# Gated linear attention with token and channel mixing: one rotating pool of eight PSUM banks, small mixing units between chunk steps, and SBUF-only work on GpSimd

## The chip, the cores and the metric

The kernel runs on one core of a Trainium2 chip. The metric is device time of one execution in microseconds (us), lower is better. The time of an execution is 2 to 3 us longer than the span of the trace that is shown beside it, because the span counts from the first to the last instruction.

Engine names in the profile: PE is TensorE (matrix products), PEld its weight loads, DVE is VectorE, ACT is ScalarE, POOL is GpSimd, SP is SyncE. A clock figure is the share of TensorE's full speed that was granted. `L172` is line 172 of the kernel in question. PSUM is the memory into which PE writes its products, here eight banks; SBUF is the working memory that holds the other tiles. An eviction is the copy of a product from PSUM to SBUF, here by VectorE or ScalarE. The line numbers of the changed kernel and of its variants differ by two or three.

## The reference

There are four batches (b = 0 to 3). Each is a gated linear attention with 8 heads, 768 time steps and head size 48, followed by a two-stage mixer with shared weights:

```python
f = 1.0 / (1.0 + np.exp(-f_logit))
for t in range(S):                                     # S = 768
    state = f[:, :, t, :, None] * state + k_t (outer) v_t
    y[:, :, t] = q_t @ state
x = y as (B, 768, 384)
h  = relu(x^T @ w_tok1) @ w_tok2                       # 768 -> 256 -> 768, over time steps
u  = x + h^T
out = u + relu(u @ w_ch1) @ w_ch2                      # 384 -> 1536 -> 384, over channels
```

Both kernels compute the recurrence in 6 chunks of 128 time steps: the logarithms of the gates (each kept as a bf16 value `Lhi` and its remainder `Llo`) are summed inside a chunk by a triangular matrix product, q and k are scaled by the exponentials of those sums (`qh`, `kh`), `qh` and `kh` are transposed on PE, their products are the scores of a chunk, and a small state is handed from chunk to chunk. `state_bd`, `x_bf` and `u_bf` are bf16 copies of the state, of the attention's output x and of the mixer's u. The mixing of batch b is computed while the attention of batch b+1 runs, so PE has two streams to interleave. The last mixing has nothing beside it.

## The kernel before

A bank of PSUM belongs to one purpose each: five to attention, three to the mixing, in turn. q, k, v and the weights are loaded (and cast to bf16) through GpSimd's queue, f through SyncE's.

```python
ps_S = pt([128, 512], FP32, "ps_S")
ps_AT = [pt([128, 4, 128], FP32, f"ps_AT{p}") for p in range(2)]
ps_y = pt(...); ps_dg = pt(...)
ps_moe = [pt([128, 512], FP32, f"ps_moe{i}") for i in range(3)]      # mixing

def g_lo():                                                          # all arithmetic on ACT and DVE
    nc.vector.tensor_tensor(Llo[ib][...], fbc, Lhi[ib][...], ALU.subtract)

def attn_chunk(b, c, mid=(), front_next=None):
    ...
    nc.vector.tensor_tensor(qh[i][:, :, 0:D], q_sb[ib][:, :, c, :], G[i][:, :, 0:D], ALU.mult)
    nc.vector.tensor_tensor(kh[i][:, :, 0:D], k_sb[ib][:, :, c, :], Gi[i][:, :, 0:D], ALU.mult)
    # PE: transposes of qh and kh to ps_AT[0], ps_AT[1]
    nc.scalar.copy(qkT[i][:, 0:4, :], ps_AT[0])
    nc.vector.tensor_copy(qkT[i][:, 4:8, :], ps_AT[1])               # L186
    # PE: scores from qkT                                            # L191
    front_next()                       # sums of the next chunk
    for m in mid: m()                  # one sixth of the previous batch's mixing
    # masking, readout, state ... (cut)

load_batch_inputs(0, 0, 2); load_batch_inputs(0, 2, NCH)             # 18 loads on GpSimd's queue
load_batch_inputs(1)                                                 # q, k, v of batch 1
load_weights()                                                       # w_tok1, w_tok2, w_ch1, w_ch2
```

## Time and profile before

The median is 242.74 us (two runs, 242.68 and 242.79). The span of the trace is 240.4 us at a mean PE clock of 0.979.

First the page of the kernel before: busy time by engine, and rows of the table of 40 slices (each digit is the busy share of 6 us in tenths).

```profile
PE 183.6 (76%) x1673; PEld 111.5 (46%) x1688; DVE 152.1 (63%) x341; ACT 137.2 (57%) x262; POOL 40.1 (17%) x39
...
PE   0413376103858999999999999999999999989993
...
POOL 9823910821302100150300000000000000000000
...
DMA  8999999999999900099490000121000002100022
```

PE is nearly always busy from slice 14 on, and busy for less than half of the time before it, while the DMA row stands at 8 to 9. So the kernel has two parts: a start held by loads, and a long stretch bound by PE.

Next the table of windows of the same run: duration, then busy time (and instructions) of PE, PEld, DVE, ACT and POOL, PE's clock, DMA share and GB/s. I cut the span where the first scores of a batch start on PE: 78.0 us for batch 1, 119.9 for batch 2, 163.6 for batch 3.

```profile
78.00:119.90 41.90, 40.03 (x401) 24.44 (x403) 35.16 (x78) 23.68 (x56) 6.92 (x4) 1.00 0.93 70
119.90:163.60 43.70, 42.09 (x419) 25.96 (x424) 33.98 (x81) 24.06 (x59) 0.48 (x1) 1.00 0.34 44
163.60:240.40 76.80, 70.09 (x575) 41.89 (x577) 44.41 (x98) 34.63 (x79) 0.00 (x0) 1.00 0.09 32
```

In batch 2's stage PE is busy 42.1 of 43.7 us. Why it idles so little can be seen in PE's timeline (start, duration, engine, line, what): between the transpose of `kh` (L184) and the scores (L191), which must wait for the eviction on VectorE, PE computes other things.

```profile
132.38 0.39 PE L184 MATMUL ps_AT_123<-ident,kh_95 128*128 128x128 bf16 x4
...
132.80 0.33 PE L215 MATMUL ps_dg<-v_sb_81,kh_95 128*128 128x96 bf16 x4
133.39 0.65 PE L280 MATMUL ps_moe_135<-uT,w_ch_75 128*128 128x384 bf16 x3 [0.25 <-DVE zT L285]
133.87 0.33 PE L280 MATMUL ps_moe_133<-uT,w_ch_75 128*128 128x384 bf16 x1
134.13 0.23 PE L191 MATMUL ps_AT_122<-qkT_97 48*128 48x128 bf16 x1
```

In the start, PE's longest wait is for the first weights, and GpSimd's timeline shows why they are late: they were issued after v of batch 1, whose issue had itself stood 11.26 us.

```profile
PE ps_moe_134 L247 <- DMA w_tok_73<-in_moe_w_tok_dram: 12.2, 1, 12.2
```

```profile
28.49 2.21 POOL L78 DMA_DIRECT2D k_sb_80<-in_k_dram  x1
41.96 2.22 POOL L79 DMA_DIRECT2D v_sb_82<-in_v_dram  x1 [11.26 <-issue]
44.17 0.83 POOL L62 DMA_DIRECT2D w_tok_73<-in_moe_w_tok_dram  x1
```

### The profile page before, as it was taken

The page shows a single profiled execution, that of the slowest core. Times are in us where ns is not written, and L with a number is a line of the kernel's source. Part 1 is how long each engine was busy: PE and PEld are TensorE (multiplying, and loading weights), DVE is VectorE, ACT ScalarE, POOL GpSimd, SP SyncE. Part 2 cuts the span into 40 slices and gives each one's busy share as a digit, 9 for nine tenths or more (in the row PEclk, how much of TensorE's full clock was granted, in tenths as well). Part 3 has the DMA queues.
Part 4 walks back from the last instruction along what each step waited for, and adds up shares of the span by engine and source line. Part 5 has one row for each costly group of instructions (what it writes and reads, how often), then busy time and mean ns, then how long its engine had stood idle before and what let it go on. Part 6 is the DMA issues. An engine that isn't in the chain of part 4 may idle for free.

```text
span 240.4 us, 4273 instructions
## 1 busy us (share of the span) xinstructions
PE 183.6 (76%) x1673; PEld 111.5 (46%) x1688; DVE 152.1 (63%) x341; ACT 137.2 (57%) x262; POOL 40.1 (17%) x39
## 2 busy tenths in 40 slices
PE   0413376103858999999999999999999999989993
PEld 0201253001535555566565555666556556546661
DVE  4323769300965999995489998637999872444221
ACT  5479999900697765870376777008776710556300
POOL 9823910821302100150300000000000000000000
PEclk9999999999965999999999999999999999999999
DMA  8999999999999900099490000121000002100022
GB/s 113 147 185 151 163 158 137 174 144 198 208 182 137 103 3 0 3 85 174 135 104 0 3 1 3 65 100 35 0 3 0 3 33 102 64 0 0 8 107 85
DMA packets 91539, 19.93 MB, mean 83 GB/s; under 512 B 80896, under 2 KB 91136, under 8 KB 91520
## 3 DMA queue, kind: packets, MB, share of 16 engines
q0 software_dynamic: 77168, 10.23, 78.3%
q1 hardware_dynamic: 14352, 9.44, 18.4%
q8 instruction: 13, 0.21, 0.4%
q14 instruction: 6, 0.05, 0.1%
HBM read 25.17 MB, written 4.72 MB: 124 GB/s over the span
## 4 chain that ended last, share of the span: by engine, by line
PE 34%; DVE 26%; DMA 15%; issue 9%; ACT 8%; POOL 7%; DVEq 0%; POOLq 0%
DMA q_sb_77<-in_q_dram 6%; DMA w_tok_73<-in_moe_w_tok_dram 6%; PE ps_moe_135 L298 5%; PE ps_moe_133 L298 5%; PE ps_moe_134 L298 5%; PE ps_moe_133 L280 3%; DMA out_dram<-out_sb_132 3%; DVE zT L285 3%; PE ps_moe_134 L280 3%; PE ps_moe_135 L280 3%; DVE u_nat L256 2%; DVE qkT_98 L186 2%; DVE AmT_99 L200 2%; DVE uT L270 2%; DVE state L225 2%
## 5 line engine op out<-in xcount | busy, mean ns | idle before, releaser
L298 PEld LDWEIGHTS <-zT 128*128 128x128 bf16 x288 | 27.7, 98 | 18.3
L280 PEld LDWEIGHTS <-w_ch_75 128*128 128x128 bf16 x288 | 26.5, 97 | 19.9 <-issue 4.5
L280 PE MATMUL ps_moe_133<-uT,w_ch_75 128*128 128x384 bf16 x96 | 22.9, 325 | 1.4 <-DVE uT L270 0.5
L280 PE MATMUL ps_moe_135<-uT,w_ch_75 128*128 128x384 bf16 x96 | 22.6, 325 | 0.8 <-DVE zT L285 0.5
L280 PE MATMUL ps_moe_134<-uT,w_ch_75 128*128 128x384 bf16 x96 | 22.2, 325 | 0.5 <-DVE zT L285 0.3
L220 ACT ACTIVATE x_nat_105<-ps_y 128x384 f32<-128x384 f32 x12 | 6.0, 499 | 24.8 <-PE ps_y L210 24.2
L298 PE MATMUL ps_moe_134<-w_ch_76,zT 128*128 128x384 bf16 x96 | 17.3, 326 | 0.0
L200 DVE TENSOR_TENSOR AmT_100<-ps_AT_122,tri_bf 128x512 bf16<-128x512 f32 x12 | 8.3, 688 | 14.2 <-PE ps_AT_123 L191 14.0
L298 PE MATMUL ps_moe_135<-w_ch_76,zT 128*128 128x384 bf16 x96 | 17.1, 326 | 0.0
L298 PE MATMUL ps_moe_133<-w_ch_76,zT 128*128 128x384 bf16 x96 | 17.1, 326 | 0.0
L287 ACT ACTIVATE zT<-ps_moe_134 128x384 bf16<-128x384 f32 x22 | 10.9, 496 | 8.0 <-PE ps_moe_134 L280 7.8
L161 PE MATMUL ps_dg<-ones_bf,Lhi_85 128*128 128x1 bf16 x40 | 3.5, 166 | 13.5 <-ACT Lhi_85 L143 6.7
L287 ACT ACTIVATE zT<-ps_moe_135 128x384 bf16<-128x384 f32 x22 | 11.0, 500 | 4.9 <-PE ps_moe_135 L280 4.8
L220 ACT ACTIVATE x_nat_104<-ps_y 128x384 f32<-128x384 f32 x12 | 5.8, 486 | 13.9 <-PE ps_y L210 13.9
L247 PE MATMUL ps_moe_134<-x_bf_106,w_tok_73 128*128 128x384 bf16 x6 | 2.5, 452 | 14.1 <-DMA w_tok_73<-in_moe_w_tok_dram 12.2
L247 PEld LDWEIGHTS <-w_tok_73 128*128 128x128 bf16 x48 | 4.6, 105 | 17.9 <-DMA w_tok_73<-in_moe_w_tok_dram 12.4
L287 ACT ACTIVATE zT<-ps_moe_133 128x384 bf16<-128x384 f32 x20 | 10.0, 500 | 4.3 <-PE ps_moe_133 L280 4.2
L224 DVE TENSOR_TENSOR state<-state,ps_dg 48x192 f32<-48x192 f32 x20 | 6.8, 342 | 8.5 <-ACT qkT_98 L185 4.9
L257 ACT ACTIVATE u_bf<-u_nat 128x384 bf16<-128x384 f32 x24 | 11.0, 519 | 1.8 <-DVE u_nat L256 1.6
L200 DVE TENSOR_TENSOR AmT_99<-ps_AT_122,tri_bf 128x512 bf16<-128x512 f32 x12 | 8.2, 685 | 6.0 <-PE ps_AT_123 L191 5.7
L175 ACT ACTIVATE glast<-ps_dg 128x4 f32<-128x4 f32 x20 | 3.6, 178 | 14.1 <-DVE state L227 12.7
L191 PE MATMUL ps_AT_122<-qkT_97 48*128 48x128 bf16 x48 | 5.1, 232 | 7.3 <-ACT qkT_97 L185 5.5
(149 smaller groups left out, 470.3 us busy)
## 6 DMA issues: line engine op xcount, KB each, us to landing
out_dram<-out_sb_131 SPq DMA_DIRECT2D x12, 192.0 KB, 1.9
out_dram<-out_sb_132 SPq DMA_DIRECT2D x12, 192.0 KB, 1.9
f_sb_83<-in_f_logit_dram SPq DMA_DIRECT2D x6, 192.0 KB, 5.7
q_sb_78<-in_q_dram POOLq DMA_DIRECT2D x2, 576.0 KB, 12.6
k_sb_80<-in_k_dram POOLq DMA_DIRECT2D x2, 576.0 KB, 18.2
v_sb_82<-in_v_dram POOLq DMA_DIRECT2D x2, 576.0 KB, 11.6
w_ch_75<-in_moe_w_ch_dram POOLq DMA_DIRECT2D x1, 1152.0 KB, 20.3
w_ch_76<-in_moe_w_ch_dram POOLq DMA_DIRECT2D x1, 1152.0 KB, 24.9
```

Of the source, the lines that this page charges most:

```text
L186: nc.vector.tensor_copy(qkT[i][:, 4:8, :], ps_AT[1])
L191: nc.tensor.matmul(ps_AT[par][:, hp, :], lhsT=qkT[i][rows, 4 + hp, :], rhs=qkT[i][rows, hp, :], start=True, stop=True)
L200: nc.vector.tensor_tensor(AmT[i][:, 0:4, :], ps_AT[0], tb4, ALU.mult)
L220: nc.scalar.activation(x_nat[ib][:, c, :], yflat, AF.Copy, bias=0.0, scale=1.0)
L224: nc.vector.tensor_tensor(state[0:D], state[0:D], ps_dg[0:D, :, 0:D], ALU.add)
L225: nc.vector.tensor_tensor(state[64:64 + D], state[64:64 + D], ps_dg[64:64 + D, :, D:2 * D], ALU.add)
L247: nc.tensor.matmul(pm[:, 0:DM], lhsT=w_tok1[:, kt, rt * 128:(rt + 1) * 128], rhs=x_bf[ib][:, kt, :], start=(kt == 0), stop=(kt == NCH - 1))
L257: nc.scalar.activation(u_bf[:, stt, :], u_nat[:, stt, :], AF.Copy, bias=0.0, scale=1.0)
L280: nc.tensor.matmul(pm[:, 0:384], lhsT=w_ch1[:, kt, cc * 128:(cc + 1) * 128], rhs=uT[:, kt, th * 384:(th + 1) * 384], start=(kt == 0), stop ...
L285: nc.vector.tensor_scalar(dst, pm[:, 0:384], 0.0, None, ALU.max)
L287: nc.scalar.activation(dst, pm[:, 0:384], AF.Relu, bias=0.0, scale=1.0)
L298: nc.tensor.matmul(pm[:, 0:DM], lhsT=zT[:, kt, tt * 128:(tt + 1) * 128], rhs=w_ch2[:, kt, :], start=(kt == 0), stop=(kt == 11))
```

## The change

The kernel was rewritten with five intentions: all PSUM tiles come from one pool of eight banks in rotation, so that neither stream is short of banks; the mixing is cut into 44 small units, spread over four places of each chunk step; the state and the sums are kept compact (384 instead of 512 columns, no padded products); a single activation table is preloaded; and work that touches SBUF alone goes to GpSimd, which was 17% busy. The weights are loaded before batch 1, and f of batch 1 goes through GpSimd's queue too.

The core of the diff, with cuts:

```diff
-    ps_S = pt([128, 512], FP32, "ps_S")
-    ps_AT = [pt([128, 4, 128], FP32, f"ps_AT{p}") for p in range(2)]
-    ...
-    ps_moe = [pt([128, 512], FP32, f"ps_moe{i}") for i in range(3)]
+    ps = ctx.enter_context(tc.tile_pool(name="ps", bufs=8, space=bass.MemoryType.PSUM))
+    def bank(name):
+        return ps.tile([128, 512], FP32, tag="bank", name=name)
+    nc.scalar.preload_act_table_set("natural_log_exp_and_others")
 ...
-            nc.scalar.activation(Lhi[ib]..., fbc, AF.Copy, bias=0.0, scale=1.0)
-            nc.vector.tensor_tensor(Llo[ib]..., fbc, Lhi[ib]..., ALU.subtract)
+        nc.vector.tensor_copy(Lhi[i]..., fbc)
+        nc.gpsimd.tensor_tensor(Llo[i]..., fbc, Lhi[i]..., ALU.subtract)
 ...
-        nc.vector.tensor_tensor(kh[i]..., k_sb[ib][:, :, c, :], Gi[i]..., ALU.mult)
+        nc.gpsimd.tensor_tensor(kh[j]..., k_sb[i][:, :, c, :], Gi[j], ALU.mult)
 ...
-        nc.scalar.activation(x_bf[ib][:, c, :], yflat, AF.Copy, bias=0.0, scale=1.0)
+        nc.gpsimd.tensor_copy(x_bf[i][:, c, :], x_nat[i][:, c, :])
+            nc.gpsimd.tensor_copy(u_bf[:, tt, :], u_nat[:, tt, :])
+        nc.gpsimd.tensor_copy(state_bd[j]..., s...)          # two of them
 ...
-    load_batch_inputs(1)
-    load_weights()
+    for w, src in ((w_tok1, ...), (w_tok2, ...), (w_ch1, ...), (w_ch2, ...)):
+        nc.gpsimd.dma_start(out=w, in_=...)
+    load_f(1, nc.gpsimd)
+    load_qkv(1)
 ...
+            scores(b, c)      # transposes, evictions, scores, masking
+            mix()             # a few units of the previous batch's mixing
+            front(b, c + 1)
+            mix()
+            update(b, c)
+            mix()
+            readout(b, c)
+            mix()
```

The kernel as changed is called "after" below.

## The prediction

> **What bounds the kernel now.** The table of windows splits the 240.4 us span into five stages. (1) 0–71 us: loading and batch 0's attention; PE is busy 26 us of it. The DMA row reads 8–9 tenths throughout, and the list of waits has PE waiting 12.2 us for w_tok until 58.2 us, because the weights were issued (44–47 us in GpSimd's timeline) behind batch 1's q, k, v. (2) 71–119.6 us: batch 1's attention with batch 0's mixing, 48.6 us, of which 10 us ran at half clock. (3) and (4) 119.6–205.2: 43.7 and 41.9 us, PE busy 96%. Start-to-start issue distances there (matmul timeline: 162 ns per 384 columns, 56 per 128) sum to about 28 us of mixing and 11 us of attention per batch, so only 3–4 us are idle. In 120–150 VectorE is 90% busy; in 150–162 PE runs the second channel product alone. (5) 205.2–240.4: the last mixing, 35.2 us, almost pure PE.
>
> **Removed.** 11 table loads of 1283 ns on ACT (about 14 us; the Trainium skill, "ScalarE: Activation LUTs", section "Table sets: the hidden batching unit", says natural_log_exp_and_others holds both functions). On VectorE per batch: kh 2.1, Llo 2.6, state casts 3.1, one state add of each pair 1.7, uT 1.7, against zT +2.2 and the Lhi cast +2: about 7 us of 34 less. ACT loses x_bf 3.0, u_bf 3.1, Lhi 2.1, some zT, and gains uT 2.9. PE loses only about 0.6 us per batch (384 instead of 512 columns in the front).
>
> **Added to GpSimd,** per batch 20–25 us. Estimate from the Trainium skill, "GPSIMD Engine Reference", section 3.1 (about 2.6 cycles per element for two inputs at 1.2 GHz): kh about 1 us against 0.35 on VectorE, Llo about 5 against 2.55. No GpSimd arithmetic of this kind is in this trace.
>
> **On the critical path.** Steady stages are PE-bound: small units let the second channel product fill VectorE-bound gaps, 43.7 to about 41 each; batch 1's stage to about 42 (less cold clock); the tail to about 33.5 (transposes by row tile start earlier). Together about 156 us after batch 1's first chunk, against 169.
>
> **The start decides.** The weights now precede batch 1's loads, which removes the 12 us wait. DMA packets: a batch's q, k or v (6144 packets) takes about 5 us alone, the weights about 17, so w_tok lands by 30 us, all weights by 43, f(1) 49, q(1) 54, k(1) 59, v(1) 64. Hence batch 1 can't start before about 60 us. But Llo and kh of batch 0 now sit on GpSimd, behind whatever DMA issues precede them there. Before, v(1)'s issue stood 11.3 us waiting ("issue") and went out only after q(1) had landed. If all 26 issues come first, GpSimd is held until about 56 us, batch 0's attention starts then, cold and GpSimd-bound, and batch 1 starts at about 85 us: total about 241. If the arithmetic slips in between, about 217. I take both as likely.
>
> **Predicted: 226 us, 8 in 10 between 208 and 246. Faster by over 2%: 0.67; within 2%: 0.16; slower by over 2%: 0.17.**
>
> **What would show it.** Right: no wait for w_tok; one table load; PE 95% or more busy from batch 1's start; VectorE under 80% busy there; that stretch 40–42 us per batch. Start: GpSimd's timeline tells whether the first Llo precedes the last load's issue; if not, PE idles to 50 us or later with GpSimd as releaser. Batch 1's first scores near 60 or 85 us.
>
> **What would make it wrong.** GpSimd elementwise much slower than the estimate, so that kh or state_bd ends chunk steps; GpSimd blocked in mid-kernel by issuing loads of batches 2 and 3 (2.2 us each); banks taken in rotation so that one slow eviction holds PE; gates of batch 1 in ACT's queue waiting for the later f(1).

## The result, and the profile after

| | median us | runs | ratio to before, 95% interval |
|---|---|---|---|
| before | 242.74 | 242.68, 242.79 | |
| after | 274.38 | 273.35, 275.4 | 1.1303 [1.1122, 1.1485] |

The change made the kernel 13% slower. A ratio here and below is the mean time of one kernel's runs over that of the other's runs of the same rounds, so it is not quite the ratio of the medians that are quoted. Executions over 1.5% slower than the fastest of the same kernel are left out of the means.

The page of the kernel after:

```profile
PE 183.5 (68%) x1768; PEld 112.3 (41%) x1768; DVE 136.1 (50%) x254; ACT 104.7 (39%) x221; POOL 122.0 (45%) x167
...
PE   0100000138857879888876788998878999889995
...
POOL 9789002795596887331945433232243323140000
```

PE does the same work (183.5 us against 183.6), VectorE and ScalarE do less, as intended, and the span is 31 us longer. PE idles through most of the first eight slices, and then stands mostly at 7 to 8 tenths where it stood at 9.

The windows, cut in the same way at the first scores of each batch (60.9, 90.9, 140.5 and 191.9 us):

```profile
0.00:60.90 60.90, 4.44 (x52) 2.55 (x54) 10.19 (x22) 14.49 (x27) 38.65 (x43) 1.00 1.83 157
60.90:90.90 30.00, 22.22 (x256) 13.36 (x256) 21.21 (x36) 20.19 (x39) 20.60 (x27) 1.00 0.61 78
90.90:140.50 49.60, 43.42 (x442) 27.01 (x442) 34.84 (x60) 20.77 (x47) 28.80 (x36) 1.00 0.82 58
140.50:191.90 51.40, 42.81 (x442) 26.81 (x442) 28.94 (x57) 20.63 (x47) 17.49 (x30) 0.97 0.49 50
191.90:271.40 79.50, 70.57 (x578) 42.58 (x578) 40.95 (x79) 28.59 (x61) 16.51 (x33) 0.98 0.09 33
```

Where the 31.0 us went, stage by stage:

| stage | before | after | difference |
|---|---|---|---|
| start, up to the first scores of batch 1 | 78.0 | 90.9 | +12.9 |
| batch 1 | 41.9 | 49.6 | +7.7 |
| batch 2 | 43.7 | 51.4 | +7.7 |
| batch 3 and last mixing | 76.8 | 79.5 | +2.7 |

**The start.** GpSimd's timeline after shows that its first arithmetic, `Llo` (L128), stands behind all 26 load issues in its order:

```profile
45.49 2.22 POOL L116 DMA_DIRECT2D k_sb_81<-in_k_dram  x1 [17.95 <-issue]
49.19 2.21 POOL L116 DMA_DIRECT2D v_sb_83<-in_v_dram  x1 [1.48 <-issue]
51.42 5.54 POOL L128 TENSOR_TENSOR Llo_88<-f_sb_84,Lhi_86 128x384 bf16<-128x384 f32 x6
...
58.52 0.90 POOL L155 TENSOR_TENSOR kh_96<-k_sb_80,Gi_92 128x384 bf16<-128x384 bf16 x1
```

The Trainium skill, "PSUM — Partial Sum Buffer", section "Engine vs sequencer instructions", calls GpSimd's queue strictly first in, first out; this trace agrees: ScalarE had finished the gates of batch 0 by 14.9 us, yet `Llo` came after the last issue, and PE's list of waits (total, times, longest) puts 39.0 us of one wait on it. In the same time ScalarE stood 30.24 us at the first gate of batch 1, because f of batch 1 was queued behind the weights:

```profile
PE pt L141 <- POOL Llo_88 L128: 40.8, 5, 39.0
```

```profile
45.12 1.58 ACT L125 ACTIVATE f_sb_85<-f_sb_85 128x768 f32<-128x768 f32 x2 [30.24 <-DMA f_sb_85<-in_f_logit_dram]
```

**The steady batches.** PE's timeline after, in batch 2: nothing stands between the transposes of `kh` (L166) and the scores (L172), so PE waits the whole eviction on VectorE.

```profile
160.34 0.39 PE L166 MATMUL pk<-ident,kh_96 128*128 128x128 bf16 x4
161.52 0.23 PE L172 MATMUL pA_1592<-qkT_98 48*128 48x128 bf16 x1 [0.79 <-DVE qkT_98 L167]
...
161.85 1.64 PE L245 MATMUL pm<-uT,w_ch_76 128*128 128x384 bf16 x9
```

In batch 2's stage this wait appears six times, once per chunk, 0.8 us each; with one wait of 3.0 us for `x_bf` and one of 0.8 us for `u_bf`, both on GpSimd, that is 8.6 of the stage's 8.6 idle us on PE (51.4 less 42.8). Before, PE idled 1.6 us there.

```profile
PE pm L222 <- POOL x_bf_111 L191: 3.0, 1, 3.0
PE pA_1940 L172 <- DVE qkT_99 L167: 0.8, 1, 0.8
```

### The profile page after: what moved, and what is told of

The parts are those of the page before. It is cut to its first block, busy times and chain, and to the rows that moved or that the text cites. A ratio compares the mean times of both kernels' runs of the same rounds, so it can differ in the third digit from the quotient of the medians.

```text
span 271.4 us, 4457 instructions
## 1 busy us (share of the span) xinstructions
PE 183.5 (68%) x1768; PEld 112.3 (41%) x1768; DVE 136.1 (50%) x254; ACT 104.7 (39%) x221; POOL 122.0 (45%) x167
## 4 chain that ended last, share of the span: by engine, by line
PE 57%; POOL 16%; DVE 11%; issue 11%; DMA 3%; ACT 1%; POOLq 0%; DVEq 0%
PE pm L245 18%; PE pm L256 18%; DMA k_sb_80<-in_k_dram 3%; PE pm L222 3%; DVE qkT_99 L167 3%; DVE qkT_98 L167 3%; POOL Llo_88 L128 3%; PE pk L166 2%; POOL u_bf L232 2%; PE pS L150 2%; PE pm L229 2%; PE py L182 2%; PE pd L200 1%; PE pS L151 1%; POOL q_sb_78 L118 1%
## 5 line engine op out<-in xcount | busy, mean ns | idle before, releaser
L245 PE MATMUL pm<-uT,w_ch_76 128*128 128x384 bf16 x288 | 53.0, 331 | 0.0
L256 PE MATMUL pm<-w_ch_77,zT 128*128 128x384 bf16 x288 | 50.0, 326 | 0.0
L251 ACT ACTIVATE zT<-pm 128x384 bf16<-128x384 f32 x48 | 23.6, 492 | 26.1 <-PE pm L245 25.7
L249 DVE TENSOR_SCALAR zT<-pm 128x384 bf16<-128x384 f32 x48 | 26.5, 554 | 11.7 <-PE pm L245 11.1
L141 PEld LDWEIGHTS <-Llo_88 128*128 128x128 bf16 x40 | 2.5, 100 | 42.0 <-POOL Llo_88 L128 41.9
L259 DVE TENSOR_TENSOR out_sb_118<-u_nat,pm 128x384 f32<-128x384 f32 x12 | 6.6, 554 | 16.3 <-PE pm L256 16.3
L232 POOL CAST u_bf<-u_nat 128x384 bf16<-128x384 f32 x24 | 11.3, 503 | 6.0 <-DVE u_nat L231 5.9
L167 DVE CAST qkT_98<-pk 128x512 bf16<-128x512 f32 x12 | 8.3, 689 | 11.0 <-PE pk L166 11.0
L155 POOL TENSOR_TENSOR kh_96<-k_sb_81,Gi_92 128x384 bf16<-128x384 bf16 x6 | 5.5, 914 | 17.8 <-ACT Gi_92 L153 13.9
L128 POOL TENSOR_TENSOR Llo_89<-f_sb_85,Lhi_87 128x768 bf16<-128x768 f32 x6 | 9.7, 1630 | 8.3 <-PE pm L245 4.3
L239 ACT CAST uT<-pm 128x384 bf16<-128x384 f32 x24 | 11.0, 479 | 6.4 <-PE pm L237 6.3
L259 DVE TENSOR_TENSOR out_sb_117<-u_nat,pm 128x384 f32<-128x384 f32 x12 | 6.6, 553 | 12.6 <-PE pm L256 10.7
L155 POOL TENSOR_TENSOR kh_97<-k_sb_80,Gi_93 128x384 bf16<-128x384 bf16 x6 | 5.6, 926 | 16.0 <-ACT Gi_93 L153 11.2
L116 POOL DMA_DIRECT2D k_sb_81<-in_k_dram x2 | 4.4, 2212 | 17.9 <-issue 17.9
L167 DVE CAST qkT_99<-pk 128x512 bf16<-128x512 f32 x12 | 8.3, 690 | 8.0 <-PE pk L166 7.9
```

The costliest lines, as they stand in the source:

```text
L128: nc.gpsimd.tensor_tensor(Llo[i][:, c0:c1, :, 0:D], fbc, Lhi[i][:, c0:c1, :, 0:D], ALU.subtract)
L155: nc.gpsimd.tensor_tensor(kh[j][:, :, 0:D], k_sb[i][:, :, c, :], Gi[j], ALU.mult)
L167: nc.vector.tensor_copy(qkT[j][:, 4:8, :], pk.rearrange("p (a t) -> p a t", a=4))
L232: nc.gpsimd.tensor_copy(u_bf[:, tt, :], u_nat[:, tt, :])
L239: nc.scalar.copy(uT[:, :, tt * 128:(tt + 1) * 128], pm[:, 0:DM].rearrange("p (m t) -> p m t", m=3))
L245: nc.tensor.matmul(pm[:, 0:384], lhsT=w_ch1[:, kt, cc * 128:(cc + 1) * 128], rhs=uT[:, kt, th * 384:(th + 1) * 384], start=(kt == 0), stop ...
```

## The experiments

Two theories were to be tested, and a third came up on the way.

- **Order of PE.** One rotating pool hands out its banks in the order in which the source asks for them. PE's order as built, which the two timelines above show too, follows the source in the kernel after, while the kernel before has mixing products moved in between. If so, a pool of its own for the mixing, or a mixing unit written between transposes and scores, removes the 0.8 us per chunk. Rival: the small units, the compact state or GpSimd's slower `kh` make the steady batches slow.
- **Start.** Arithmetic on GpSimd stands behind the load issues. Rival: the new place of f, on a queue behind the weights, is the cause; or the start is bound by bytes, whatever the order.

All fifteen runs below (fourteen kernels, one of them run twice) gave correct results. They ran in four calls, each with runs of the kernel before on the same chip (medians 242.05, 242.81, 242.72 and 242.66 us). The stage times are from the profiled run of each.

| run | median us | ratio to before, 95% interval | first scores of batch 0, 1 | batch 1 | batch 2 | batch 3 and tail |
|---|---|---|---|---|---|---|
| before | 242.74 | | 16.1, 78.0 | 41.9 | 43.7 | 76.8 |
| after | 274.38 | 1.1303 [1.1122, 1.1485] | 60.9, 90.9 | 49.6 | 51.4 | 79.5 |
| two_pools | 258.89 | 1.0690 [1.0662, 1.0718] | 61.8, 93.8 | 45.1 | 45.2 | 73.2 |
| mix_between | 259.68 | 1.0706 [1.0666, 1.0745] | 61.2, 92.0 | 44.7 | 47.3 | 73.6 |
| b0_off_pool | 269.60 | 1.1149 [1.1085, 1.1212] | 18.3, 82.7 | 54.3 | 51.3 | 79.5 |
| f1_sync | 277.55 | 1.1409 [1.1362, 1.1455] | 64.7, 94.6 | 51.5 | 51.5 | 78.4 |
| b0_off_f1 | 260.07 | 1.0699 [1.0646, 1.0752] | 18.0, 68.3 | 58.8 | 52.2 | 78.4 |
| no_pool_f1 | 256.70 | 1.0541 [1.0485, 1.0598] | 18.0, 66.6 | 54.0 | 51.3 | 83.4 |
| b0_off_f1_pools | 244.35 | 1.0061 [1.0009, 1.0113] | 17.9, 71.8 | 52.8 | 45.6 | 73.5 |
| no_pool_f1_pools | 236.23 | 0.9719 [0.9680, 0.9759] | 18.0, 69.2 | 47.3 | 42.6 | 75.0 |
| no_pool_pools | 242.93 | 1.0011 [0.9995, 1.0026] | 18.6, 78.2 | 45.3 | 42.7 | 74.6 |
| before_pool_arith | 266.11 | 1.0974 [1.0933, 1.1015] | 53.9, 89.2 | 52.1 | 44.7 | 78.0 |
| before_w_first | 239.67 | 0.9883 [0.9863, 0.9904] | 16.1, 74.0 | 43.0 | 43.7 | 76.9 |
| ch_weights_late | 228.09 | 0.9401 [0.9374, 0.9428] | 18.2, 62.4 | 46.6 | 42.6 | 75.1 |
| before_llo_pool | 249.97 | 1.0303 [1.0275, 1.0330] | 16.1, 68.0 | 57.8 | 43.7 | 76.9 |
| ch_weights_late_again | 228.48 | 0.9407 [0.9381, 0.9433] | 17.8, 61.4 | 46.2 | 42.6 | 75.1 |
| pool_last | 226.77 | 0.9354 [0.9328, 0.9380] | 18.0, 62.7 | 47.9 | 42.7 | 73.6 |

### PE's order: two_pools and mix_between

The first gives the mixing three banks of its own, the second writes one of the four mixing places between the transposes and the scores. Nothing else changes.

```diff
     def bank(name):
+        if name == "pm":
+            return ps.tile([128, 512], FP32, tag="mixbank", name=name, bufs=3)
-        return ps.tile([128, 512], FP32, tag="bank", name=name)          # of 8
+        return ps.tile([128, 512], FP32, tag="bank", name=name, bufs=5)
```

> The changed kernel with one edit: mixing takes its PSUM banks from a tag of its own with 3 banks, everything else rotates through the other 5. Built, its PE queue now has channel-product matmuls between the transposes of a chunk and its scores, where the changed kernel has none. Theory A (the shared rotation pins PE to the order in which banks are asked for, so PE stands 0.8 us in every chunk step while VectorE evicts the transposed k): the 0.79 us waits of PE for qkT vanish in batches 1 to 3, a batch falls from about 49.5 to about 44 us, the whole from 274 to about 258. Rival B (GpSimd's slower arithmetic and its load issues hold the chunk steps): less than 5 us faster, batches stay at 48 or more. The start (first scores of batch 1 at 90.9 us) stays in both.

```diff
-            scores(b, c)
-            mix()
+            turn(b, c)        # transposes and evictions
+            mix()
+            scores(b, c)      # scores and masking
```

> The changed kernel with one edit: still one pool of 8 banks, but the first of the four calls that add mixing units to a chunk step stands between the transposes and the scores instead of after the scores. Theory A (only the missing PE work between transposes and scores costs the time in the batches): as two_pools, about 44 us per batch and about 258 in all. If instead the number of banks for mixing or their rotation costs the time, the qkT wait goes but another wait takes its place and the total stays above 268. Rival B (GpSimd): no gain.

Both gained about 15 us (258.89 and 259.68 against 274.38), by two different edits that share little but PE's order. PE's timeline of two_pools shows five mixing products where there was a hole:

```profile
155.73 0.39 PE L168 MATMUL pk<-ident,kh 128*128 128x128 bf16 x4
155.95 0.98 PE L247 MATMUL pm<-uT,w_ch 128*128 128x384 bf16 x5
156.90 0.40 PE L174 MATMUL pA<-qkT 48*128 48x128 bf16 x8
```

The wait of the scores for `qkT` in the two steady batches of two_pools is down to 1.1 us in all. So most of the steady loss is PE's order; the small units and the compact state are the same in these kernels and in the kernel after. What remains in batch 2 (45.2 us against 42.8 busy) is mostly a wait of 2.0 us for `x_bf` on GpSimd. The last stage is now 3.6 us shorter than before (73.2 against 76.8); the prediction's 41 for batch 3 and 33.5 for the last mixing had made it 74.5.

### The start: b0_off_pool, f1_sync, b0_off_f1

b0_off_pool takes the arithmetic of batch 0 alone off GpSimd; f1_sync moves only f of batch 1 to SyncE's queue; b0_off_f1 does both.

```diff
-        nc.gpsimd.tensor_tensor(Llo..., ALU.subtract)
+        (nc.vector if b == 0 else nc.gpsimd).tensor_tensor(Llo..., ALU.subtract)
         # the same for kh and state_bd; x_bf of batch 0 on ScalarE
```

> The changed kernel with the arithmetic of batch 0 alone taken off GpSimd (Llo, kh, state casts to VectorE, x_bf to ACT); batches 1 to 3 as they were. Theory C (batch 0 starts late because Llo and kh stand in GpSimd's queue behind all 26 load issues, the last at 49 us): the first chunk starts at about 10 us instead of 51; then ACT's queue stands at the gates of batch 1 until f(1) lands at about 45 us, so batch 1's first scores come at about 70 us instead of 90.9 and the total falls to about 253. Rival D (the data of batch 0 and the weights are what is late, or ACT's wait for f(1) alone holds everything): the first scores of batch 0 stay at 45 us or later, and the total falls by less than 8 us.

```diff
-    load_f(1, nc.gpsimd)
+    load_f(1, nc.sync)
```

> The changed kernel with one edit: the load of batch 1's f goes back to the SyncE queue, as in the kernel before; batch 0's arithmetic stays on GpSimd. Rival D (ACT waiting 30 us for f(1) is what starts batch 0 late): batch 0 starts at about 25 us, total about 250. Theory C: ACT's wait goes but GpSimd still issues 25 loads first; [...] the last issue moves from 49 to about 42 us, and the total falls by only about 5 to 8 us, to about 267.

> Both start edits together: batch 0's arithmetic off GpSimd and f(1) loaded by SyncE, one pool of 8 banks. Alone the first moved batch 1's first scores from 90.9 only to 82.7 us and the second to 94.6 us. Theory C2 (the start waits for whichever of two queues frees last: GpSimd's, held by load issues until 51 us, and ACT's, held by f(1) until 45 to 51 us; removing one leaves the other): together the first scores of batch 1 come at about 61 us (GpSimd still has Llo and kh of batch 1 behind its last load issue at about 51), the batches stay at 50 to 51 us, total about 242. Rival E (the loads themselves, in the new order, set the start): first scores of batch 1 stay at 78 us or later, total above 258.

Alone, neither edit helps much. With batch 0 off GpSimd its first scores come at 18.3 us instead of 60.9, but ScalarE then stands at the gates of batch 1, 18.1 us for f, until 51.2 us, and the first scores of batch 1 come at 82.7 (269.60 us in all). With f on SyncE, v of batch 1 is held 17.31 us, GpSimd's first `Llo` starts at 53.3 us, and the kernel is no faster than after (277.55; the intervals of the two ratios overlap). Both totals missed what was expected, about 253 and about 267 us; that f1_sync would issue its last load at 42 us was wrong, it did so at 51.1. Only both together bring the first scores of batch 1 to 68.3 us (about 61 expected). The start has two queues in series, GpSimd's and ScalarE's, and each hides the other.

But b0_off_f1 took 260 us where about 242 were expected: of the 22.6 us gained up to batch 1, 9.2 were given back in batch 1 (58.8 us against 49.6) and 0.8 in batch 2. Part of that was a cold clock (0.55 of full speed from 80 to 90 us); the next runs look for the rest.

### All arithmetic off GpSimd, and the parts left out one by one

no_pool_f1 takes all arithmetic off GpSimd and puts f of batch 1 on SyncE. no_pool_f1_pools gives the mixing its own banks as well. b0_off_f1_pools keeps GpSimd's arithmetic for batches 1 to 3. no_pool_pools is no_pool_f1_pools with f of batch 1 back on GpSimd's queue.

```diff
-        nc.gpsimd.tensor_tensor(Llo...) / nc.gpsimd.tensor_tensor(kh...) / nc.gpsimd.tensor_copy(state_bd...)
+        nc.vector.tensor_tensor(Llo...) / nc.vector.tensor_tensor(kh...) / nc.vector.tensor_copy(state_bd...)
-        nc.gpsimd.tensor_copy(x_bf...) / nc.gpsimd.tensor_copy(u_bf...)
+        nc.scalar.copy(x_bf...) / nc.scalar.copy(u_bf...)
```

> As b0_off_f1, but all arithmetic of all batches off GpSimd (Llo, kh, state casts on VectorE; x_bf, u_bf on ACT), one pool of 8 banks. Theory A (PE's fixed order costs the batches, GpSimd's slower arithmetic does not): batches stay at 49 to 51 us although kh falls from 0.9 to 0.35 us; first scores of batch 1 at about 58 us; total about 240. Rival B (GpSimd's latency and load issues cost the batches): batches fall to 46 us or less, total below 228.

> b0_off_f1 and two_pools together. If the start and the order of PE are two separate losses they add: 242 minus 15 to 16, about 226, which beats the kernel before (242). If the two are one loss seen twice: no less than 236.

> no_pool_f1 and two_pools together. With PE's order freed, what GpSimd takes off VectorE and ACT should now show: theory, about 9 us of VectorE work per batch return, VectorE is near 38 of 44 us, a batch takes 44 to 46 us, total about 225 to 230, the same as b0_off_f1_pools within 2%. If GpSimd's share was worth having, this one is slower by 5 us or more; if it was a burden, faster by 5 us or more.

> The best kernel so far (no arithmetic on GpSimd, f of batch 1 on SyncE, own banks for the mixing, 236.2 us) with f of batch 1 put back on GpSimd's queue, as the change has it: what that one move costs once the rest is mended. Theory (ACT stands in order at the gates of batch 1 until f has landed, about 51 us as in the run with batch 0 alone taken off GpSimd): the first scores of batch 1 at about 80 us instead of 69, total 245 to 248 us. Rival (the queue of f matters only together with GpSimd arithmetic): first scores within 3 us of 69, total within 3 us of 236.

All four totals missed. Expected were about 240 us for no_pool_f1 (256.70 measured), about 226 for b0_off_f1_pools (244.35), 225 to 230 for no_pool_f1_pools (236.23) and 245 to 248 for no_pool_pools (242.93). The second had a test: about 226 us if the start and PE's order are separate losses, no less than 236 if they are one. By its letter they would be one, but it had taken 242 us for b0_off_f1. From the measured 260.07, less the 15.5 us that two_pools gained, one gets 244.6 us, and 244.35 were measured: the two losses add, and the miss was already in b0_off_f1. By the test of the third, GpSimd's arithmetic was a burden (over 5 us; 8.1 measured).

no_pool_f1_pools, at 236.23 us, was the first to beat the kernel before. Around it, each part can be left out singly:

- Without its own banks (no_pool_f1): 20.5 us more. PE waited 9.4 us in 11 waits for `qkT` from VectorE in batches 1 and 2, with no arithmetic on GpSimd at all, so these waits do not come from GpSimd. Part of the 20.5 us goes with the clock: the profiled run had a mean of 0.960 against 0.998, and from the first scores of batch 1 on PE was busy 9.0 us longer and idle 14.8 us longer.
- With f of batch 1 on GpSimd's queue (no_pool_pools): 6.7 us more; the first scores of batch 1 at 78.2 instead of 69.2 us. ScalarE waited 18.4 us for f until 52.0 us.
- With GpSimd's arithmetic in batches 1 to 3 (b0_off_f1_pools): 8.1 us more. It is not the clock: one run of b0_off_f1_pools at a mean clock of 0.972 took 243.33 us, and one of no_pool_f1_pools at 0.964 took 236.05. (The profiled run of b0_off_f1_pools, whose stages the table shows, had 0.84 in batch 1.)

Why the last one costs can be read in GpSimd's timeline of b0_off_f1_pools. The loads of batch 2 are issued from the same queue as `kh`, the issue of v stood 9.12 us, and `kh` of the next chunk stood behind it; PE waited 9.12 us for that `kh`.

```profile
80.36 2.21 POOL L118 DMA_DIRECT2D v_sb<-in_v_dram  x1 [9.12 <-issue]
82.59 0.92 POOL L157 TENSOR_TENSOR kh<-k_sb,Gi 128x384 bf16<-128x384 bf16 x1
```

In the last stage, where no loads are issued, b0_off_f1_pools is 1.5 us faster than no_pool_f1_pools (73.5 against 75.0).

### The same questions asked of the kernel before: before_pool_arith and before_w_first

before_pool_arith is the kernel before with `Llo` and `kh` on GpSimd, nothing else.

```diff
-            nc.vector.tensor_tensor(Llo[ib]..., ALU.subtract)
+            nc.gpsimd.tensor_tensor(Llo[ib]..., ALU.subtract)
-        nc.vector.tensor_tensor(kh[i]..., ALU.mult)
+        nc.gpsimd.tensor_tensor(kh[i]..., ALU.mult)
```

> The kernel before with one part of the change alone: Llo and kh on GpSimd. In the built order of GpSimd the first Llo then stands behind all 25 load issues (18 of batch 0, 3 of batch 1, 4 of the weights), as in the change. Theory (arithmetic behind loads in GpSimd's order is what broke the start): the first scores move from 16 us to about 50 (the last weight's issue ended at 47.4 us before), the first scores of batch 1 from 78 to about 88, and the kernel takes 253 to 260 us. Rival (the start was broken by the new order of the loads and the one pool, GpSimd's arithmetic only waited along): first scores of batch 1 within 4 us of 78 and a total within 5 us of 242.7.

The start behaved as the theory said: first scores at 53.9 and 89.2 us (expected about 50 and 88). So this one part of the change breaks the start by itself, in a kernel with the old loads and the old banks. The total, 266.11 us, lies above the expected 253 to 260, because batch 1 took 52.1 us instead of 41.9 (the clock in it was 0.93, and PE waited 6.1 us in one piece for an eviction on VectorE). VectorE's and GpSimd's timelines of this run show something that neither theory had: a product of 0.35 us took 4.69 us while `Llo` ran on GpSimd.

```profile
112.36 4.69 DVE L227 TENSOR_TENSOR state<-state,glast 128x192 f32<-128x192 f32 x1
```

```profile
112.19 4.65 POOL L146 TENSOR_TENSOR Llo<-f_sb,Lhi 128x2304 bf16<-128x2304 f32 x1
```

before_w_first is the kernel before with the weights loaded before batch 1's q, k, v, which is the order of the change.

```diff
-    load_batch_inputs(1)
-    load_weights()
+    load_weights()
+    load_batch_inputs(1)
```

> The kernel before with the weights loaded ahead of batch 1's q, k, v, nothing else. The prediction took the 12 us wait for w_tok as time to be gained. If so: no wait for w_tok over 3 us, the first scores of batch 1 at about 66 to 70 instead of 78, total about 232 to 236 us. Rival (the start is bound by the bytes of both batches and the weights, whichever comes first, and the wait only moves to q, k or v of batch 1): the first scores of batch 1 within 3 us of 78, total 240 to 244 us.

It fell between: first scores of batch 1 at 74.0 instead of 78.0 us, 239.67 us, a ratio of 0.9883. The 12.2 us wait for `w_tok` became one of 6.5 us, and v of batch 1 was now held 23.7 us, until 62.3 us. So most of the wait only moved to other loads. The clock from 60 to 74 us was 0.50 in this run, and from 71 to 78 us it was 0.53 in the kernel before; what that cost in each was not separated.

### GpSimd arithmetic holding VectorE: before_llo_pool

> The kernel before with one thing on GpSimd: Llo of batches 1, 2 and 3 (three instructions, 2304 elements wide, about 4.6 us each by the run before_pool_arith; nothing of batch 0). VectorE loses 7.7 us of work. Theory (GpSimd's instruction holds VectorE instructions that take two inputs from SBUF until it ends): in each of the three places a qh, a kh or a state times glast product, 0.35 us otherwise, takes 2 to 4.7 us, and the total rises by 1 to 8 us over 242.7. Rival (GpSimd costs only its place behind load issues): those products stay at 0.35 to 0.4 us throughout, and the total stays within 1 us of 242.7 or falls.

```diff
-            nc.vector.tensor_tensor(Llo[ib]..., ALU.subtract)
+            (nc.vector if b == 0 else nc.gpsimd).tensor_tensor(Llo[ib]..., ALU.subtract)
```

Three instructions moved, and VectorE was held in all three places. Its timeline, and GpSimd's:

```profile
44.55 7.88 DVE L230 CAST state_bd<-state 48x192 bf16<-48x192 f32 x1
...
77.89 5.67 DVE L177 TENSOR_TENSOR qh<-q_sb,G 128x384 bf16<-128x384 bf16 x1
...
101.52 6.37 DVE L227 TENSOR_TENSOR state<-state,glast 128x192 f32<-128x192 f32 x1
```

```profile
47.74 4.56 POOL L146 TENSOR_TENSOR Llo<-f_sb,Lhi 128x2304 bf16<-128x2304 f32 x1
...
78.77 4.56 POOL L146 TENSOR_TENSOR Llo<-f_sb,Lhi 128x2304 bf16<-128x2304 f32 x1
...
103.11 4.55 POOL L146 TENSOR_TENSOR Llo<-f_sb,Lhi 128x2304 bf16<-128x2304 f32 x1
```

Each of the three VectorE instructions ends 0.1 to 0.2 us after `Llo` does (at 52.4, 83.6 and 107.9 us against 52.3, 83.3 and 107.7). The two products take at most 0.36 us in the kernel before, and this cast (L230) at most 0.26 us. The Trainium skill, "SBUF — State Buffer", section "Who interferes with whom", says this: VectorE's second read port is GpSimd's only one, it is held for a whole instruction, and a VectorE instruction with two inputs from SBUF, or in one of its fast copy modes, contends with a GpSimd instruction that reads SBUF. The trace agrees for the two products, which have two inputs from SBUF; whether the cast ran in a fast copy mode no run shows. The cast began 3.2 us before `Llo`, while the loads of the weights were issued. The other cast of the state (L229) was held in the kernel before too, with no arithmetic on GpSimd: 2.06 us instead of 0.25, from 26.37 us, and it ended 0.1 us after the issue of q of batch 1 (26.11 to 28.35 us). In before_pool_arith the same cast took 1.84 and 1.56 us, each time to the end of a load issue. So a load issue held a cast as well, with nothing else on GpSimd. None of these holds was in the prediction.

The total rose by 7.3 us, inside the expected 1 to 8. It is not a clean measure of the hold, though: in the compiled streams PE's order had changed as well, the first scores of batch 1 came 10 us earlier, and batch 1 took 15.9 us longer, at a clock of 0.88 against 1.00. What is shown is the hold; its price alone is not.

In the kernel after, `Llo` is cut into thirds of a batch (768 wide, 1.63 us), so a hold is shorter: the `state` times `gl` product (L209) took 0.40 to 0.87 us in the mean, by buffer, and `qh` 0.36 to 0.72, against 0.35 without GpSimd's arithmetic. What that cost on the critical path was not measured apart from the queue.

### Loads in order of need, and GpSimd where no loads are left: ch_weights_late and pool_last

ch_weights_late is no_pool_f1_pools with the channel weights, which are needed last, loaded after batch 1's q, k, v.

```diff
-    # loads of w_tok1, w_tok2, w_ch1, w_ch2
     load_f(1, nc.sync)
+    # loads of w_tok1, w_tok2
     load_qkv(1)
+    # loads of w_ch1, w_ch2
```

> The best kernel so far (236.2 us, the first scores of batch 1 at 69 us, GpSimd's issue of v of batch 1 held until 63.5 us) with w_ch1 and w_ch2 loaded after batch 1's q, k, v; w_tok1 and w_tok2 stay ahead of them. If the order of the loads decides when batch 1 starts: first scores at 58 to 62 us, total 227 to 231 us. Rival (the bytes are needed before 72 us in any order, so a wait for w_ch takes the place of the wait for k): PE waits 5 us or more for w_ch and the total stays at 234 to 238 us.

> The best kernel so far once more, for the comparison with pool_last on the same chip: 228 us, batch 3 with the tail 75.1 us.

It took 228.09 us, and 228.48 when run again; the first scores of batch 1 came at 62.4 and 61.4 us. v of batch 1 was held 7.0 us instead of 22.9. No wait for the channel weights took the place of the old one. PE's wait of about 11 us for `w_tok` stayed (10.8 us here, 11.2 in no_pool_f1_pools), so the start is still held by loads.

pool_last puts back on GpSimd what no load can hold up: `kh`, `x_bf` and `state_bd` of batch 3, and `u_bf` of the last two mixings.

```diff
-        nc.vector.tensor_tensor(kh...)
+        (nc.vector if b < B - 1 else nc.gpsimd).tensor_tensor(kh...)
         # the same for state_bd; x_bf and u_bf from ScalarE to GpSimd likewise
```

> The best kernel so far (ch_weights_late), with kh, x_bf and state_bd of the last batch and u_bf of the last two mixings on GpSimd, where no load is left to issue. Theory (GpSimd arithmetic costs time only where loads share the queue or wide instructions hold VectorE): the last batch with the tail 73.3 to 74.2 us instead of 75.1, total 226.3 to 227.5 us. Rival (GpSimd's slower kh, 0.91 against 0.35 us, costs wherever it stands): the last batch with the tail 76 us or more, total over 228.5 us.

The last stage took 73.6 us instead of 75.1, as the theory said, and the median is 226.77 us, the best of all, 6.5% below the kernel before. Against ch_weights_late_again (228.48) the gain is 0.7%, at the edge of what these runs can tell: the two intervals, [0.9328, 0.9380] and [0.9381, 0.9433], just fail to overlap. Its profiled run was the slowest of six: in it the first scores of batch 1 came 1.3 us later and batch 1 took 1.7 us longer than in ch_weights_late_again, where the edit changes nothing.

## Why the prediction was wrong

The prediction was 226 us with a range of 208 to 246, and a chance of 0.67 for faster; measured were 274.38 us. Point by point:

- **The step that failed first: "small units let the second channel product fill VectorE-bound gaps, 43.7 to about 41 each".** Measured were 49.6 and 51.4 us. The units were small, but they stood only after the scores in the source, and with one rotating pool PE's order stayed that of the source. A hole of 0.8 us per chunk opened in front of the scores that the old kernel had filled. two_pools and mix_between, which change little but that order, recovered 15 us. Even with the order mended and GpSimd's arithmetic gone, the best steady batch took 42.6 us (no_pool_f1_pools), of which PE was busy 41.9: the expected gain of 2.7 us was too large as well, since PE was idle for only 1.6 of the 43.7 us before. The prediction named "banks taken in rotation so that one slow eviction holds PE" as a danger; the rotation did it, but through the order and not through a bank that came free late.
- **The start: the bad branch came true.** The prediction gave two branches and took both as likely. All 26 issues came first; the first `Llo` started at 51.4 us (56 predicted), batch 1's first scores came at 90.9 us (about 85). The sum "about 241" for this branch failed by the steady part: 85 + 156 = 241 against 90.9 + 49.6 + 51.4 + 79.5 = 271.4 us of span. So of the 30 us by which even the bad branch was short, about 6 are the start and 24 the stages after it. The 226 lies between the two branches; the bad branch could have been read from the change, since nothing in its source puts arithmetic of batch 0 before a load issue in GpSimd's order.
- **"This removes the 12 us wait": mis-sized.** Done alone in the kernel before, it was worth 3 us (before_w_first): the wait shrank to 6.5 us, and v of batch 1 was held 23.7 us instead. The order of the loads does count, though: with only the channel weights put last, ch_weights_late gained 8.1 us over no_pool_f1_pools.
- **Cost of GpSimd's arithmetic: right.** The Trainium skill, "GPSIMD Engine Reference", section 3.1, gives about 2.6 cycles per element for two inputs; estimated from that were about 1 us for `kh` and about 5 us for a batch of `Llo`. Measured: `kh` 0.91 us, `Llo` 4.55 to 4.65 us in one piece, and three times 1.63 us in thirds. What was not in the sum is what that arithmetic does beside its own time: it waits behind loads, and it holds VectorE.
- **"GpSimd blocked in mid-kernel by issuing loads (2.2 us each)": right in kind, too small.** An issue itself took 2.2 us, but the stand before one was up to 9.12 us in b0_off_f1_pools. In the kernel after, GpSimd's `x_bf` came late behind such an issue and PE waited 3.0 us.
- **"Gates of batch 1 in ACT's queue waiting for the later f(1)": right.** ScalarE stood 30.24 us. It was worth 6.7 us once the rest was mended (no_pool_pools), and hidden before.
- **Removed work: right and worth little by itself.** There is one table load instead of eleven of 1.283 us, as the skill's "ScalarE: Activation LUTs", section "Table sets: the hidden batching unit", had it; VectorE's busy time fell from 152 to 136 us and ScalarE's from 137 to 105. PE's work was the same to 0.1 us, and PE is what bounds the steady stages.
- **The tail: right once PE's order was mended.** The last stage fell from 76.8 to 73.2 us in two_pools.

What stays open: what GpSimd waits for when it stands before a load issue (not VectorE: in the kernel after VectorE was not busy at all from 27.6 to 45.4 us, while k of batch 1 was held); how much of GpSimd's 8 us in batches 1 to 3 is the queue behind loads and how much the hold of VectorE; and why two products of before_llo_pool were already held 0.9 and 1.6 us before `Llo` began, while GpSimd was still issuing a load.

## What to carry to other kernels

A shared rotating buffer pool is also an order: before two streams of work are put on one pool, look at what the built order of the busiest engine puts between a producer and the consumer that waits for its eviction, and give each stream its own buffers, or write the filler there. An engine that issues loads is not idle, even where it is 17% busy: arithmetic placed behind its issues inherits every stand of the load path. Here it paid to keep it off until the last load was out, and to load in the order of need. When two queues in series hold a start, mending either alone can show little; test both together before a theory is dropped.

## What the Trainium skill lacked or had wrong

- "DMA: Bandwidth & Descriptors" (sections "Anatomy of one DMA — SWDGE (gpsimd) path" and "Issuing engines are not separate DMA queues") calls the generation of descriptors "small, variable" and the time to initiate a DMA usually small relative to the DMA itself. Here one q, k or v load of a whole batch (576 KB) took GpSimd 2.2 us to issue, and the stand before such an issue was 11.3 us (before), 17.95 us (after) and up to 23.7 us (before_w_first). Neither section says that GpSimd can stand there (VectorE was idle through the 17.95 us), nor that arithmetic behind it in its queue stands too (PE waited 39.0 us in one piece for such arithmetic after).
- "GPSIMD Engine Reference", section 3.1: the 2.6 cycles per element held within a tenth (0.91, 1.63 and 4.55 us for 384, 768 and 2304 elements; estimates from it at 1.2 GHz are 0.83, 1.66 and 4.99). What is lacking beside it is a warning that such arithmetic also pays for its place in the queue: PE waited 9.12 us for one `kh` behind a held load in b0_off_f1_pools.
- "SBUF — State Buffer", section "Who interferes with whom": the hold while `Llo` ran was as described. Two products of two SBUF inputs were held from 0.9 and 1.6 us before the GpSimd arithmetic began, during a load issue (5.67 and 6.37 us in all, against 4.56 of `Llo`). The page infers that such products and descriptor generation use different sides of the shared ports, and the kernel before agrees (at most 0.36 us, beside load issues too); what holds them when arithmetic is next in the queue no page that was read says.
- No page that was read has it that one rotating PSUM pool for two streams kept PE in source order in this kernel: 0.8 us per chunk step, about 15 us of 274.
